# A constant group for eps in bn_aggr, and q's diagonal copies on GpSimd

## The chip, the cores and the metric

The kernel runs on one core of a Trainium2 chip. A core has five engines that run side by side, each with its own list of instructions taken strictly in order: TensorE (PE, matrix products; its weight loads appear as PEld), VectorE (DVE), ScalarE (ACT), GpSimd (POOL) and SyncE (SP), which here only starts transfers. Engines wait for each other on semaphores. The metric is the device time in microseconds (us) of one execution.

## The reference

The input x is 2048 tokens of 448 numbers in bf16. Six vectors of 448 (shift, scale and gate, twice) come from a small conditioning vector c. Then there are two residual blocks:

```python
mod = (_silu(c) @ w_mod).reshape(1, 6, 1, -1)      # sa, ca, ga, sb, cb, gb
h = _layernorm(x) * (1 + ca) + sa
x = x + ga * _A_ref(h, A_wqkv, A_wo)
h = _layernorm(x) * (1 + cb) + sb
x = x + gb * _B_ref(h, B_w_in, B_w_sp, B_b_sp, B_w_out)
```

Block A is attention with 16 heads of 28 numbers, in which a token sees itself and the 255 tokens before it. Block B multiplies by w_in (448 to 1792), applies gelu, splits into z1 and z2, normalizes z2 over its 896 numbers, mixes it over the tokens with a 2048x2048 matrix w_sp, adds b_sp, multiplies with z1 and multiplies by w_out (896 to 448). Each normalization is `(x - m) / jnp.sqrt(v + eps)` with eps = 1e-5, over 448 numbers in the two `h` and over 896 in z2, so each needs a mean and a variance for every token, 3 x 2048 in all.

## The kernel before

Tokens lie on the 128 partitions: 16 tiles of 128 tokens, in four blocks of four tiles (`tb`, 0 to 3). The work of each engine is written out as one list of small operations, `PLAN`. A word such as `d166` puts operation 166 on DVE; p is PE, a is ACT, d is DVE, t is POOL, s is SP. Each engine gets its operations in the order of the words. The class `Sched` turns what an operation depends on into semaphore waits, also on the engine's own earlier operations, PE's excepted. No planner runs when the program is built: the list alone sets the order.

**Statistics and normalization.** `stats` (L623) writes, for each tile, one `bn_stats` (L626; two for z2, by halves) and one `bn_aggr` (L629) on DVE, which gives mean and variance in `mv_all`. An addition of eps (L631) on DVE or POOL writes `ve_all`. POOL raises it to the power -0.5 (L633) into `rs_all`. `norm` (L636) applies both, on DVE in one operation (L644), or with a negated product of mean and `rs_all` first (L649, stored in `ve_all` too), and then an operation on POOL or DVE (L651). The three slots of `st_all`, `mv_all`, `rs_all` are those of the first norm, the second norm and z2. For z2 the operation that applies them is L1135.

**q, k, v.** The normalized rows `xn` of a block are transposed into `hT` by four transfers that SP starts (L467; for block 0 PE transposes), then scaled and shifted by DVE, POOL or ACT (L732 in blocks 1 to 3: four operations, each of which needs all four transfers). PE makes q (L763, block 0: L797), k (L821) and v (L841). ACT or DVE takes each out of PSUM (L772, L773, L802, L803 for q, L833 and L834 for k, L845 and L846 for v).

**q's diagonal blocks.** `QBD` is a second, block-diagonal layout of a part of q, with which PE scores a few keys of several heads in one matmul. For each block of tokens ACT fills it with zeros once per buffer (L521); there are two buffers, used by turns. Then four copies follow, one for each group of 32 partitions: 32 partitions x 256 elements in block 0 (L815 on ACT, L816 on DVE), 32 x 512 in the others (L790 on ACT, L791 on DVE). A copy needs all evictions of q of its block. Thirteen of the sixteen are on DVE, three on ACT. PE's L967, once per tile from tile 2 on, reads `QBD` and waits for all four copies of the tile's block: blocks 0, 1, 2 and 3 are first used at tiles 2, 4, 8 and 12.

**Attention and after.** For each tile PE makes scores (L956, L967; the first two tiles L926), ACT takes exponentials into `PW` (L912), DVE multiplies by a mask into `PT` (L975), PE multiplies with v (L1003), DVE divides (L1017, L1019), SP transposes `o_sb`, PE multiplies by wo (L1029), DVE adds to x (L1033). The second norm, its transposes (L467), the scaling L1054, the products L1123 (z2) and L1144 (z1) follow. When all of z2 is normalized, PE mixes over tokens (L1168) and multiplies by w_out (L1187); that is the last part, from 158 us on.

These lines hold the steps that the change touches: L623 to L657, L675 (`lock_q`), L782 to L791, L808 to L816, and `order` (L157).

Of the kernel before, what the change touches and what calls it, by code (L numbers as in the profile page):

```python
# [6 lines left out]
F32 = mybir.dt.float32  # L7
# [5 lines left out]
d24 d22 p47.1 p56.3 p48.2 p55.0 p57.1 p59.0 a0 a3 a5 a7 a9 d23 p37.1 p65.2 p71.3 p61.1 p49.0 p64.2 p50.3 p73.0  # L13
p46.3 p67.0 s1 s2 s4 d110 s6 s10 s8 a38 p42.0 p43 p44.1 p45 p70.2 p72.1 p60.2 t27 t28 t29 t32 t33 t30 d108
d111 t31 d109 t112 t113 t34 a100 t26 t102 t35 d115.3 d114.2 p124.7 d83 d82 p127.0 p75.0 a128 a129 d103 d125
d126 d118 d119 d116 d117 a104 p80.1 p77.0 p78.1 p76.2 p74.0 p52.3 p69.2 p68.0 s12 d182 d180 p62.1 t101 p51.0
p148.1 p81.2 p139.5 p140 p149 a150 p79.1 p54.2 a141 t106 t107 t105 p136.7 p137 a138 p63.2 t120 t121 d123.2
d122.0 p133.3 p130.6 p66.3 p53.0 p145.0 p146 p58.2 a131 d176 d183 d134 a135 s13 d243 d178 d177 d181 d179 t25
d184 t185 t191 t187 t189 d245 d41 d241 d186.3 s11 p142.7 p372.0 a132 p163.1 p170.6 p171 d244 p164 d165 a147
p151.0 p143 d144 d172 d247 p152 d153 a373.0 p378.0 p154.1 p155 d156 a39 a379.4 p397.0 a398.1 a399 a169 t36  # L20
d382 d374 d246 d166 d376 p157.7 p158 a159 s15 p90.1 p91 d92 d248 d84 d85 d242 d400 p93.0 p94 d95 d380 s193
t188.1 s194 t190.2 s195 t192.0 s196 d197 d200 p404.0 a405.5 p173.1 p174 a175 p160.7 p161 p375.0 p86.0 p87 d88
d198 d89 a406 a40 p425.0 a426.6.0 t249 t250 t254 d407 t252 t199 p377 p381 p383 d409 d384 d402 t253.2 d162
p217.0 p218 a219 a168 p210.1 p211 d212 p433.0 a434.0 p201.0 p202 a203 d167 p204.1 p205 a206 s14 d310 d385.2
p401.0 p403 p453.0 a454.2.1 s16 d430 s849 s259 t255.1 s260 d251.0 d256 d429 d436 d312 s386 s258 t257.3 s261
t97 t96 t262 t99 t263 t265 p226.0 p427.0 a428 p207.1 p227 p408 p208 d228 d306 p410 d411 d412.1 d307 s413 d98
d311 d435 a209 d215 d458 p461.0 p229.0 a462.1 d464 d214 d463 d457 p220.1 p221 p230 a231 p431.0 p432 s851
p481.0 p437 p438 d439 p223.0 p224 d225 d313 p455.0 a222 p232.1 d440.2 s441 d213 a482.3.2 d486 p489.0 d308 p233
d234 p235.0 p236 a456 a216 p483.0 p459.0 p460 a490.0 p508.0 d491 d492 d309 s21 s17 s852 p465 p466 d467 d485
d468.0 s469 a237 t264 p387.0 p388 d389 p414.1 p415 a484 p510.0 d416 t314 t315 a509.6.0 p536.0 a511 d390 d512  # L30
d391 p487.0 p488 p493 p494 p272.0 p538.0 d495 d496.1 a537.2.1 d541 d513 d540 p273 a274 p516.0 a517.5 p269.1
p275.0 p276 d277 p270 d271 p514.0 p515 a539 p564.0 a565.3.2 p282.0 p266.1 p267 a268 d519 p283 p566.0 a567 a284
d518 p520 t319 t320.1 s325 t321 t322.2 s326 d316.0 s323 t317 t318.3 s324 t330 d280 d417 d569 p544.0 a545.1
p442.1 p443 d444 d281 p521 d522 d523.0 p288.0 p289 a290 p291.1 p292 a293 p572.0 a573.5 p238.0 p239 d279 p294.1
p542.0 p295 p543 p592.0 a240 p470.0 p471 d445 d446 d546 d418 d419 d278 s20 s497 s848 s524 t392 t393 d547
d394.2 t395 s396 a296 a593.4.0 d568 p548 p549 p285.1 p594.0 p286 a287 p600.0 a601.2 d575 d472 p300.0 p301 a302
d550 d551.1 p570.0 p571 d596 d574 d473 p576 p577 p619.0 t420 t329 t327 d328 d597 p525.1 p337.0 p526 d578
d579.0 p598.0 a595 p599 p338 d603 d474 d527 a620.3.1 p627.0 d602 d528 d475 d421 d529 d530 t531 t447 t476
t422.0 t532 p340.1 p341 a339 s552 p553.0 p554 s18 p604 p605 a628.5 p647.0 a648.6.2 p621.0 a622 d342 p498.1
# [24 lines left out]
p1047.3 p1048 a1068 p1054.0 a1069 p1055.1 p1056 p1049 a1051 a1050 a1052 a1059 p1057 a1060 a1061 a1053 a1058
d1009 d992 d1002 d1008 d1001 d1010 d959 d1003 t1004 t1011 t1012 d880 d941 d952 d970 d977 d1013 d887 s846 s840
s845 s847 s838 s862 s839 s869 s863 s868 t1005 d1006 d988 t993 t994 d995 p1121.4 p1085.5 s837 p1070.1 d1071.1
d1122.0 t1072 p1082.2 p1124.4 t1123 p1076.7 d1077.0 t1078 d1083.0 t1084 p1115.3 d1116.0 t1117 s857 s854 s856
s867 s859 s861 s864 s855 s865 s860 s866 p1157.7 p1106.2 d1158.0 d1086.1 t1087 t820 t814 t1159 p1154.0 d1155.1
t1156 p1118.7 d1119.1 t1120 p1190.3 d1191.1 t1192 d1107.1 t1108 d1125.1 p1112.6 p1172.7 d1113.0 t1114 t1126
p1079.4 p1073.6 d1080.1 p1187.1 t816 t1081 d1074.0 t1075 d1173.0 p1109.6 p1148.2 p1088.4 p1175.0 p1184.7  # L70
d1089.1 t1090 d1110.1 p1094.4 p1181.6 t1111 p1130.5 t1174 d1188.0 p1178.1 d1095.3 d1149.1 p1127.2 d1131.0
t1189 d1179.0 p1136.3 p1097.1 p1091.4 t1180 d1176.0 s1132 d1137.0 t1150 p1139.5 s1096 d1185.1 d1128.3 t1186
d1092.2 s1093 d1182.1 t1183 d1140.1 t1141 p1103.4 d1104.1 s1105 d1098.1 s1129 s1099 p1142.7 p1151.5 p1145.0
d1143.1 t1144 d1146.1 t1177 p1201.2 p1100.1 t1147 p1197.4 d1152.0 t1153 s1138 d1101.0 s1102 p1202 d1203.0
s1204 p1205.0 p1206 d1207.2 s1208 p1160.3 p1163.6 d1164.0 d1161.1 s1162 s1165 p1193.5 p1194 p1198 d1195.3
s1196 p1133.2 d1199.0 d1134.2 s1135 s1200 p1166.5 d1167.3 s1168 p1169.3 d1170.1 s1171
"""


class Hold:  # L80


    def __init__(self, res):
# [1186 lines left out]
```

## Time and profile before

| what | value |
|---|---|
| device time, median of 3 runs | 282.59 us (282.34 to 283.21) |
| span of the profiled execution, first to last instruction | 279.0 us; no device time of that execution is given beside it |
| PE busy | 267.3 us (96%) |
| DVE busy | 164.5 us (59%) |
| POOL busy | 127.3 us (46%) |
| ACT busy | 121.4 us (44%) |
| copies into QBD on DVE | 13: 11 of 32x512, median 284 ns; 2 of 32x256, median 200 ns |
| additions of eps (L631) | 22 on POOL, median 232 ns; 15 on DVE, median 147 ns |

How to read the rows: L975 is line 975 of the kernel; `out<-in` names what an instruction writes and reads, x56 how many there are. A row of the timeline starts with its start and its length in us; several instructions of one kind that stand together are one row, and their lengths overlap a little, since an engine starts one before the one ahead has fully ended. `[1.02 <-DVE KT L834]` says that the engine was idle for 1.02 us before it and what ended the wait. SPq is SP's queue. A row of waits gives total us, times, longest. PE's busy time is modelled from its starts, so a busy PE is not PE at its peak.

### The profile page before, as it was taken

To read this page: it belongs to the slowest core of one execution; us is meant where nothing else is said; L and a number is where in the kernel's file an instruction comes from. 1 tells how busy PE (TensorE), PEld (TensorE's weight loads), DVE (VectorE), ACT (ScalarE), POOL (GpSimd) and SP (SyncE) were. 2 spreads that over 40 slices of the span, in tenths; PEclk is the share of its full clock that TensorE was granted. 3 is DMA by queue.
4 is the path that set the end of the run, shared out by engine and by line. 5 is a ranking of instruction groups with operands and counts; after the bars stand their busy time and mean duration, and the time that the engine had idled before them with its cause. 6 is when DMAs were issued, how large, how long until landed. Compare 5 with 4: busy or idle time off the path is not lost.

```text
span 279.0 us, 8426 instructions
## 1 busy us (share of the span) xinstructions
PE 267.3 (96%) x3741; PEld 155.6 (56%) x3751; DVE 164.5 (59%) x377; ACT 121.4 (44%) x142; POOL 127.3 (46%) x182
## 2 busy tenths in 40 slices
PE   7899998998999799999989899999999999999995
PEld 5786686677668676544545444444444444454552
DVE  3698999978999999938879501120212012153143
ACT  2399998899699789466755500000000000000000
POOL 7554567617364831596576503155363024062320
PEclk9999999999999999999999999999999999999999
DMA  7997953956632343659489996000000000102013
GB/s 203 294 238 136 147 100 97 121 93 97 126 62 50 98 80 61 179 89 150 99 153 192 212 182 130 0 0 0 2 1 0 0 2 0 33 16 62 0 39 115
DMA packets 67302, 25.55 MB, mean 92 GB/s; under 512 B 58497, under 2 KB 66178, under 8 KB 67266
## 3 DMA queue, kind: packets, MB, share of 16 engines
q1 hardware_dynamic: 66304, 24.21, 43.6%
q10 hardware_dynamic: 962, 0.80, 1.1%
q8 instruction: 29, 0.48, 0.7%
q14 instruction: 7, 0.06, 0.1%
HBM read 9.01 MB, written 1.84 MB: 39 GB/s over the span
## 4 chain that ended last, share of the span: by engine, by line
PE 53%; DVE 21%; POOL 12%; DMA 7%; ACT 3%; issue 2%; SPq 1%; POOLq 0%; DVEq 0%
PE ps L1168 34%; DVE PT L975 8%; PE ps L1187 8%; POOL rs_all L633 5%; DMA hT<-xn 5%; DVE st_all L626 3%; DMA wmodA<-in_w_mod_dram 2%; DVE o_sb L1019 2%; DVE x_sb L1033 2%; PE ps L763 2%; POOL hT L1054 2%; POOL ve_all L631 2%; PE ps L956 1%; PE ps L821 1%; PE ps L841 1%
## 5 line engine op out<-in xcount | busy, mean ns | idle before, releaser
L1175 POOL TENSOR_TENSOR z1T<-tmpg,z1T 128x512 bf16<-128x512 bf16 x28 | 32.0, 1152 | 74.5 <-DVE tmpg L1172 74.5
L1172 DVE TENSOR_TENSOR tmpg<-ps,bsp_bc 128x512 bf16<-128x512 f32 x28 | 19.0, 689 | 75.6 <-PE ps L1168 64.3
L912 ACT ACTIVATE PW<-ps 128x2048 bf16<-128x2048 f32 (+1 forms) x42 | 60.0, 1454 | 6.8 <-PE ps L956 5.2
L1168 PE MATMUL ps<-wspB,z 128*128 128x512 bf16 x219 | 49.7, 379 | 0.3
L1168 PE MATMUL ps<-wspA,z 128*128 128x512 bf16 x219 | 49.1, 379 | 0.9 <-DVE z L1135 0.7
L975 DVE TENSOR_TENSOR PT<-PW,mask 128x1024 bf16<-128x1024 bf16 x56 | 38.6, 714 | 0.1
L1168 PEld LDWEIGHTS ps<-wspA,z 128*128 128x128 bf16 x224 | 21.8, 98 | 27.2 <-DVE z L1135 1.0
L1168 PEld LDWEIGHTS ps<-wspB,z 128*128 128x128 bf16 x224 | 21.9, 98 | 26.2
L633 POOL TENSOR_TENSOR rs_all<-ve_all,neghalf 128x1 f32<-128x1 f32 (+2 forms) x37 | 24.5, 670 | 19.4 <-DVE ve_all L631 18.3
L1003 PE MATMUL ps<-Vaug,PT 128*128 128x32 bf16 x496 | 23.4, 177 | 1.3 <-DVE PT L975 0.7
L1003 PEld LDWEIGHTS ps<-Vaug,PT 128*128 128x128 bf16 x496 | 21.5, 96 | 3.9 <-DVE o_sb L1019 1.0
L1123 PE MATMUL ps<-w_in,hT 64*128 64x448 bf16 x224 | 22.0, 349 | 1.2 <-DVE st_all L626 1.2
L1144 PE MATMUL ps<-hT,w_in 64*128 64x512 bf16 x196 | 22.2, 376 | 0.0
L1187 PE MATMUL ps<-w_out_g,z1T 128*128 128x448 bf16 (+2 forms) x119 | 22.0, 342 | 0.0
L626 DVE BATCH_NORM_STATS2 st_all<-x_sb 128x6 f32<-128x448 bf16 x32 | 19.5, 617 | 3.0 <-DMA x_sb<-in_A_x_dram 2.8
L626 DVE BATCH_NORM_STATS2 st_all<-z 128x6 f32<-128x448 bf16 x32 | 18.5, 610 | 3.7 <-ACT z L1130 3.6
L1003 PE MATMUL ps<-Vaug,PW 128*128 128x32 bf16 x224 | 19.8, 176 | 0.0
L821 PE MATMUL ps<-hT,WQK 112*128 112x128 bf16 x256 | 17.4, 219 | 1.3 <-DVE KT L834 1.0
L1197 DVE TENSOR_TENSOR fin<-ps,x_sb 128x448 bf16<-128x448 f32 (+2 forms) x17 | 9.8, 595 | 14.7 <-PE ps L1187 9.9
L1003 PEld LDWEIGHTS ps<-Vaug,PW 128*128 128x128 bf16 x224 | 17.5, 96 | 1.1
L956 PE MATMUL ps<-qT,KT 32*128 32x128 bf16 (+5 forms) x1344 | 17.1, 197 | 1.0 <-DVE KT L834 0.9
L1130 ACT ACTIVATE z<-ps 128x896 bf16<-128x896 f32 x16 | 13.9, 914 | 9.3 <-PE ps L1123 6.8
(104 smaller groups left out, 361.8 us busy)
## 6 DMA issues: line engine op xcount, KB each, us to landing
out_dram<-fin SPq DMA_DIRECT2D x15, 112.0 KB, 1.7
wmodB<-in_w_mod_dram SPq DMA_DIRECT2D x1, 1568.0 KB, 14.9
x_sb<-in_A_x_dram SPq DMA_DIRECT2D x3, 448.0 KB, 9.0
w_in<-in_B_w_in_dram SPq DMA_DIRECT2D x3, 448.0 KB, 4.5
w_out_g<-in_B_w_out_dram SPq DMA_DIRECT2D x1, 784.0 KB, 5.0
bsp_bc<-in_B_b_sp_dram SPq DMA_DIRECT2D x1, 512.0 KB, 5.2
x_sb<-in_A_x_dram SPq DMA_DIRECT2D x2, 224.0 KB, 5.1
hT<-xn SPq DMA_TRANSPOSE x28, 3.2
```

The costliest lines, as they stand in the source:

```text
L626: st = [dve(0.62 if True else 0, lambda e, t=t, ci=ci, s=s: e.bn_stats(st_all[:, slot, t, ci, :], s()), deps(t), prio) for ci, s in enumer ...
L633: return pool(0.4 + 0.15 * len(tiles), lambda e: e.tensor_tensor(rs_all[:, slot, a:b], ve_all[:, slot, a:b], neghalf[:, 0:b - a], ALU.pow) ...
L821: km = lambda g, kc, start, stop, h=h, t=t: lambda e: e.matmul(ps[:, h.slot[0], g * 128:(g + 1) * 128], lhsT=WQK[0:CP, kc, 16 + 4 * g:20 + ...
L912: ex = act(xdur, lambda e, out_ap=out_ap, in_ap=in_ap: e.activation(out_ap(), in_ap(), ACT.Exp, scale=SCALE), [s] + list(after), v - 8.0 + ...
L956: fm.append(lambda e, hm=hm, qi=qi, key=key, kn=kn, lo=lo, hi=hi, col=col, p0=p0, t=t, j=j: e.matmul(ps[p0:p0 + kn, hm.slot[t], col:col + ...
L975: return lock_d(0.68, lambda e: e.tensor_tensor(cols(hp.slot[0] * 2048 + 1024 * k, [[256, 4], [128, 2], [1, 128]]), cols(at_w() + pad + at ...
L1003: fns.append(lambda e, hp=hp, hO=hO, hi=hi, bi=bi, kb=kb, hd=hd, nb=nb, a=at[hi][bi], p_of=p_of: e.matmul(ps[:, hO.slot[0], 32 * hd:32 * h ...
L1123: return lambda e, kc, p0, start, stop: e.matmul(ps[:, hs[t % 2].slot[hf], 0:D], lhsT=hT[p0:p0 + 64, kc, t * 128:(t + 1) * 128], rhs=w_in[ ...
L1144: return lambda e, kc, p0, start, stop: e.matmul(ps[:, hs[b // 2].slot[b % 2], :], lhsT=w_in[p0:p0 + 64, kc, ft * 128:(ft + 1) * 128], rhs ...
L1168: m = pe(16 * MMS, [lambda e, h=h, si=si, ft=ft, tb=tb: e.matmul(ps[:, h.slot[0], :], lhsT=z2[:, si, ft * 128:(ft + 1) * 128], rhs=(wspA i ...
L1175: u = pool(1.16, lambda e, ht=ht, ft=ft, tb=tb: e.tensor_tensor(z1T[tb][:, ft, :], tmpg[:, ht.slot[0], :], z1T[tb][:, ft, :], ALU.mult), [ ...
L1187: return [lambda e, ft=ft: e.matmul(ps[:, h.slot[0], 0:hi - lo], lhsT=z1T[t // 4][:, ft, (t % 4) * 128:(t % 4 + 1) * 128], rhs=w_out_g[:, ...
```

## The change

Two edits. First, eps no longer has an operation of its own. `bn_stats` leaves groups of three numbers (count, mean, sum of squares about the mean), and `bn_aggr` joins groups. The statistics of a tile now lie in 15 numbers; the last three are a constant group with count 0, mean 0 and a sum of squares of n times eps (n is 448 or 896), set once at the start by three memsets on DVE. `bn_aggr` reads 9 numbers (15 for z2) and its variance already holds eps. All 37 additions go, and POOL's L633 waits for `bn_aggr` itself. The negated products get a tile of their own, `nm_all`.

Second, the thirteen copies into `QBD` that were on DVE are on POOL. They use 32 of the 128 partitions; an operation so marked (`part`) waits for the operation ahead of it in POOL's list, and the one behind waits for it. The three copies on ACT stay.

`PLAN` keeps the order of its words apart from the operations that are gone or new; `d` became `t` for the thirteen copies, and all numbers are counted anew. So PE's, ACT's and SP's lists are what they were. DVE's list loses the thirteen copies and 15 additions and gains three memsets. POOL's loses 22 additions and gains the copies at these places: one ahead of the first block's three `xn` operations (L651, tiles 5 to 7); one between the `xn` operations of the next block; three ahead of the last scaling L732 of block 2; four behind the scaling L732 of block 3 and ahead of the first `rs_all` of the second norm; of the last four one ahead of an `xn` operation of the second norm (L651), two behind it, and one behind a copy L657, ahead of an `rs_all`.

```diff
+        self.part = False
...
-            self.prog[op.eng].append(op)
+            prog = self.prog[op.eng]
+            if op.eng == "pool" and prog and (op.part or prog[-1].part):
+                op.deps.add(prog[-1])
+            prog.append(op)
...
-    st_all, _, _ = alloc("st_all", [128, 3, NT, 2, 6], F32)
+    st_all, _, _ = alloc("st_all", [128, 3, NT, 15], F32)
-    ve_all, _, _ = alloc("ve_all", [128, 3, NT], F32)
+    nm_all, _, _ = alloc("nm_all", [128, 3, NT], F32)
...
+    t_eps = [dve(0.1, lambda e: e.memset(st_all[:, :, :, 12:14], 0.0), prio=-98.0),
+             dve(0.1, lambda e: e.memset(st_all[:, 0:2, :, 14:15], D * EPS), prio=-98.0),
+             dve(0.1, lambda e: e.memset(st_all[:, 2:3, :, 14:15], FH * EPS), prio=-98.0)]
...
-            st = [dve(0.62 if True else 0, lambda e, t=t, ci=ci, s=s: e.bn_stats(st_all[:, slot, t, ci, :], s()), deps(t), prio)
+            n = len(srcs(t))
+            st = [dve(0.62, lambda e, t=t, o=12 - 6 * (n - ci), s=s: e.bn_stats(st_all[:, slot, t, o:o + 6], s()), deps(t), prio)
                   for ci, s in enumerate(srcs(t))]
-            n = len(st)
-            aggr.append(dve(0.2, lambda e, t=t, n=n: e.bn_aggr(mv_all[:, slot, t, :], st_all[:, slot, t, 0:n, :]), st, prio - 0.01))
+            aggr.append(dve(0.2, lambda e, t=t, n=n: e.bn_aggr(mv_all[:, slot, t, :], st_all[:, slot, t, 12 - 6 * n:15]), [st, t_eps], prio - 0.01))
-        fe = lambda e: e.tensor_scalar(ve_all[:, slot, a:b], mv_all[:, slot, a:b, 1], EPS, None, ALU.add)
-        ve = add({"dve": (0.16, fe), "pool": (0.23, fe)}, aggr, prio)
-        return pool(0.4 + 0.15 * len(tiles), lambda e: e.tensor_tensor(rs_all[:, slot, a:b], ve_all[:, slot, a:b], neghalf[:, 0:b - a], ALU.pow),
-                    [ve, t_nh], prio - 0.01)
+        return pool(0.4 + 0.15 * len(tiles), lambda e: e.tensor_tensor(rs_all[:, slot, a:b], mv_all[:, slot, a:b, 1], neghalf[:, 0:b - a], ALU.pow),
+                    [aggr, t_nh], prio - 0.01)
...
     def lock_q(*a):
-        return locks(either(*a))
+        op = locks(free(*a))
+        op.part = True
+        return op
```

More of the change, by code (lines that the diff above doesn't have):

```diff
@@ L18 @@
[L18 to L27, printed above, removed]
@@ L73 @@
[L73 to L76, printed above, removed]
+d24 d22 p50.1 p59.3 p51.2 p58.0 p60.1 p62.0 a0 a3 a5 a7 a9 d23 d25 d26 d27 p40.1 p68.2 p74.3 p64.1 p52.0 p67.2
@@ new lines @@
+p53.3 p76.0 p49.3 p70.0 s1 s2 s4 d113 s6 s10 s8 a41 p45.0 p46 p47.1 p48 p73.2 p75.1 p63.2 t30 t31 t32 t35 t36
+t33 d111 d114 t34 d112 t115 t37 a103 t29 t105 t38 d117.3 d116.2 p125.7 d86 d85 p128.0 p78.0 a129 a130 d106
+d126 d127 d120 d121 d118 d119 a107 p83.1 p80.0 p81.1 p79.2 p77.0 p55.3 p72.2 p71.0 s12 d183 d181 p65.1 t104
+p54.0 p149.1 p84.2 p140.5 p141 p150 a151 p82.1 p57.2 a142 t109 t110 t108 p137.7 p138 a139 p66.2 t122 d124.2
+d123.0 p134.3 p131.6 p69.3 p56.0 p146.0 p147 p61.2 a132 d177 d184 d135 a136 s13 d243 d179 d178 d182 d180 t28
@@ new lines @@
+a451 a216 p477.0 p454.0 p455 a484.0 p501.0 d485 d486 d308 s21 s17 s834 p460 p461 d462 d479 d463.0 s464 a237
+t263 p385.0 p386 d387 p411.1 p412 a478 p503.0 d413 t313 a502.6.0 p528.0 a504 d388 d505 d389 p481.0 p482 p487
+p488 p271.0 p530.0 d489 d490.1 a529.2.1 d533 d506 d532 p272 a273 p509.0 a510.5 p268.1 p274.0 p275 d276 p269
+d270 p507.0 p508 a531 p555.0 a556.3.2 p281.0 p265.1 p266 a267 d512 p282 p557.0 a558 a283 d511 p513 t317 t318.1
+s323 t319 t320.2 s324 d314.0 s321 t315 t316.3 s322 t328 t279 d414 d560 p536.0 a537.1 p438.1 p439 d440 t280
@@ new lines @@
+p595 a617.5 p635.0 a636.6.2 p610.0 a611 d340 p492.1 p493 d547 p296.0 p297 a298 t471 d596 d597.2 d612 p614.0
+d613 s835 s571 s598 d494 t419 s420 d640 d548 d619 d549 d618 d495 t443 t444 t445.1 t446 s447 p662.0 a663.0.0
+d667 p615 p332.0 p333 a334 p329.1 p330 a331 d639 t343 t472.2 d473 s474 p643.0 a644.1 p599.0 p600 p637.0 a638
+p345.1 p346 p620 a347 d601 d602 t344 d645 d666 t342 p670.0 a671.2 p621 p664.0 d622 d496 p348.0 p349 a350
+p357.1 p358 t550 t551 t552.0 t804 d623.2 s624 p689.0 d646 d673 d525.2 p302.0 p303 d304 d672 s19 p641.0 p642
@@ new lines @@
+p1004.0 p1005.1 p1006 p1007 a1011 a1009 a1010 a1008 t860 t794 s795 t818 d817 t816 d891 d815 d881 d939 d927
+d899 d928 d945 t914 t876 d877 d921 t908 d909 t882 d923 p948.2 p949.3 p950 p951 p964.1 p965.0 p966 a952 d929
+d953 d954 a958 d959 d955 d883 d960 t892 t956 d893 t940 p967 a968 a974 p1028.3 p1029.1 p1030 p1031 t866 t930
+t946 t924 t800 a1032 a1033 p1012.2 p1013.3 p1014 a1034 p1020.0 a1035 p1021.1 p1022 p1015 a1017 a1016 a1018
+a1025 p1023 a1026 a1027 a1019 a1024 d976 d961 d970 d975 d969 d977 d931 d971 t978 d861 d915 d925 d941 d947 d979
@@ new lines @@
+d867 s828 s822 s827 s829 s820 s844 s821 s851 s845 s850 t972 d973 d957 t962 d963 p1087.4 p1051.5 s819 p1036.1
+d1037.1 d1088.0 t1038 p1048.2 p1090.4 t1089 p1042.7 d1043.0 t1044 d1049.0 t1050 p1081.3 d1082.0 t1083 s839
+s836 s838 s849 s841 s843 s846 s837 s847 s842 s848 p1123.7 p1072.2 d1124.0 d1052.1 t1053 t802 t796 t1125
+p1120.0 d1121.1 t1122 p1084.7 d1085.1 t1086 p1156.3 d1157.1 t1158 d1073.1 t1074 d1091.1 p1078.6 p1138.7
+d1079.0 t1080 t1092 p1045.4 p1039.6 d1046.1 p1153.1 t798 t1047 d1040.0 t1041 d1139.0 p1075.6 p1114.2 p1054.4
@@ new lines @@
+p1141.0 p1150.7 d1055.1 t1056 d1076.1 p1060.4 p1147.6 t1077 p1096.5 t1140 d1154.0 p1144.1 d1061.3 d1115.1
+p1093.2 d1097.0 t1155 d1145.0 p1102.3 p1063.1 p1057.4 t1146 d1142.0 s1098 d1103.0 t1116 p1105.5 s1062 d1151.1
+d1094.3 t1152 d1058.2 s1059 d1148.1 t1149 d1106.1 t1107 p1069.4 d1070.1 s1071 d1064.1 s1095 s1065 p1108.7
+p1117.5 p1111.0 d1109.1 t1110 d1112.1 t1143 p1167.2 p1066.1 t1113 p1163.4 d1118.0 t1119 s1104 d1067.0 s1068
+p1168 d1169.0 s1170 p1171.0 p1172 d1173.2 s1174 p1126.3 p1129.6 d1130.0 d1127.1 s1128 s1131 p1159.5 p1160
@@ L77 @@
+p1164 d1161.3 s1162 p1099.2 d1165.0 d1100.2 s1101 s1166 p1132.5 d1133.3 s1134 p1135.3 d1136.1 s1137
 """
@@ L647, in norm @@
         else:
-            nm = ve_all[:, slot, t:t + 1]
+            nm = nm_all[:, slot, t:t + 1]
             fm = lambda e: e.tensor_scalar(nm, m, z, -1.0, ALU.mult, ALU.mult)
```

84 lines of the change are left out of this document (32 added, 52 removed).

## The prediction

> **What bounds the kernel now.** I read the page first (busy shares), then the chain that ended last in order of time, busy time by stage, PE's waits, and the timeline of each engine around the instructions that move.
>
> ```profile
> span 279.0 us, 8426 instructions
> PE 267.3 (96%) x3741; PEld 155.6 (56%) x3751; DVE 164.5 (59%) x377; ACT 121.4 (44%) x142; POOL 127.3 (46%) x182
> 44.00:64.00 20.00, 20.00 (x608) 15.03 (x606) 18.33 (x41) 17.61 (x19) 9.85 (x13) 1.00 0.70 117
> 64.00:111.00 47.00, 44.73 (x1340) 32.75 (x1342) 44.76 (x95) 40.37 (x39) 23.05 (x33) 1.00 0.44 81
> 158.10 10.74 PE ps L1168 x49
> ```
>
> From 158.10 us on, TensorE (PE) works through a fixed list to the end, so the result is decided by how late it reaches that row. Before it, attention (about 28 to 111 us) has PE, VectorE (DVE) and ScalarE all nearly full. In 44 to 64 PE is busy 20.00 of 20.00 us (in the two rows by stage: length, then PE, PEld, DVE, ACT and POOL busy), in 64 to 111 DVE 44.76 of 47.00. So work taken off DVE can help only after 64, and any pause of PE in 44 to 64 is lost. These are PE's own waits, nearly all that a gain could come from after 28 us (in us: total, times, longest):
>
> ```profile
> PE ps L1123 <- DVE st_all L626: 1.2, 1, 1.2
> PE ps L821 <- DVE KT L834: 1.0, 1, 1.0
> PE ps L956 <- DVE KT L834: 0.9, 1, 0.9
> PE ps L1168 <- DVE z L1135: 0.7, 1, 0.7
> PE ps L1003 <- DVE PT L975: 0.7, 1, 0.7
> PE ps L1003 <- DVE o_sb L1019: 0.6, 1, 0.6
> ```
>
> **The change, part by part.** I keep one running number: how late PE is against the trace above. The prices first.
>
> ```profile
> L791 DVE COPY QBD<-qT x11: 269/284/753, 38.3 to 93.0; 32x512 bf16<-32x512 bf16 x11
> L615 POOL COPY WQK<-wq_st x5: 556/560/561, 8.3 to 11.3; 112x448 bf16<-112x448 bf16 x5
> L657 POOL COPY xn<-xn x13: 231/238/2659, 65.1 to 136.5; 128x64 bf16<-128x64 bf16 x13
> L975 DVE TENSOR_TENSOR PT<-PW,mask x56: 615/681/1411, 32.1 to 112.7; 128x1024 bf16<-128x1024 bf16 x56
> L631 POOL TENSOR_SCALAR ve_all<-mv_all x22: 208/232/921, 5.1 to 155.5; 128x1 f32<-128x1 f32 x18, 128x2 f32<-128x2 f32 x2, 128x4 f32<-128x4 f32 x2
> L629 DVE BATCH_NORM_AGGREGATE mv_all<-st_all 128x2 f32<-128x6 f32 x32 | 5.2, 170 | 0.3
> L629 DVE BATCH_NORM_AGGREGATE mv_all<-st_all 128x2 f32<-128x12 f32 x16 | 2.7, 186 | 0.0
> 63.15 0.75 POOL L631 TENSOR_SCALAR ve_all<-mv_all 128x1 f32<-128x1 f32 x1
> 63.99 0.57 POOL L633 TENSOR_TENSOR rs_all<-ve_all,neghalf 128x1 f32<-128x1 f32 x1
> ```
>
> Rows by source line give min/median/max in ns. GpSimd (POOL) copies 448 elements a partition in 0.56 us and 64 in 0.23, that is 0.85 ns an element, so the copy of 512 costs 0.61 us and that of 256 0.39 us. The lower bound is DVE's own 0.28, the upper one what a stretched copy shows (2.66). I take 0.61, nearest the 448-element row. POOL waiting for itself costs 0.1 us: L631 ends at 63.90, L633, which reads it, starts at 63.99 (start and length lead the timeline's rows).
>
> *Eps by a constant group.* 37 additions go, 22 on POOL and 15 on DVE. bn_aggr reads 9 or 15 numbers in place of 6 or 12; six more cost 16 ns, so three cost 8, and 48 times 8 ns is 0.4 us, taken as nothing apart from DVE's savings. Three memsets stand in DVE's list before the first statistics, while DVE waits for x: nothing; without that cover, 0.3 us. Below nothing they can't go. What the missing additions are worth is in step 5.
>
> *The copies.* Thirteen leave DVE and stand in POOL's list. PE, ACT and SP keep their lists, so it matters what POOL's in-order list then holds up.
>
> *Step 1, first block (two copies of 256).* The first copy now stands ahead of POOL's xn x3 and needs all four evictions of q.
>
> ```profile
> 19.04 2.10 POOL L651 TENSOR_SCALAR xn<-x_sb,rs_all,ve_all 128x448 bf16<-128x448 bf16 x3
> 21.75 0.68 DVE L803 CAST qT<-ps 128x512 bf16<-128x512 f32 x1
> 18.46 6.18 SPq L467 DMA_TRANSPOSE hT<-xn  x4
> DMA to landing us min/median/max: 2.5/3.3/4.0
> 25.89 0.74 DVE L732 TENSOR_SCALAR hT<-hT,modT 112x512 bf16<-112x512 bf16 x2
> 28.14 1.05 PE L821 MATMUL ps<-hT,WQK 112*128 112x128 bf16 x16
> ```
>
> The copy starts after 21.75+0.68=22.43, and xn at about 23.0 in place of 19.04. Three xn at 0.70 follow; SP issues a transpose per 1.3 us, so three more start at 23.8, 25.1, 26.4. The last of before ran to 18.46+6.18=24.64 and landed about 25.9, just when DVE's L732 began: no slack. (The landing row is of the last two.) Now it lands at 26.4+2.5=28.9. Behind SP's three queue a load of x, wo_g and a transpose of wspA, which have slack. DVE stands still at L732, its three scalings (two in the 0.74 of that row, a third after a short copy) take an estimated 1.3 us, and PE's L821 starts at 30.3, not 28.14: **2.2 late**. Bounds: 2.0 (a copy as short as DVE's) to 4.6 (4.0 to land, xn stretched).
>
> *Step 2, second block (three copies of 512).*
>
> ```profile
> 43.51 1.07 PE L821 MATMUL ps<-hT,WQK 112*128 112x128 bf16 x16 [1.02 <-DVE KT L834]
> 43.97 0.27 DVE L791 COPY QBD<-qT 32x512 bf16<-32x512 bf16 x1
> 44.41 0.38 PE L967 MATMUL ps<-QBD,KT 128*128 128x256 bf16 x2
> 44.03 1.45 POOL L732 TENSOR_SCALAR hT<-hT,modT 112x512 bf16<-112x512 bf16 x1
> ```
>
> PE's wait of 1.02 absorbs some, since DVE has shed copies: 1.2 late at 43.51. But L967 needs every copy of its block; DVE finished at 44.24, PE used it at 44.41. On POOL the three stand where the last L732 began, 44.03, and POOL's stage is some 1.9 late from step 1 (its last xn waits for DVE, late by 2.2 less one copy): 44.03+1.9+3x0.61+0.3=48.1. PE's L967 starts at 48.2: **3.8 late**, and PE is full until 64. Bounds: 2.2 (POOL's scalings unstretched) to 6.
>
> *Step 3, third block (four copies).*
>
> ```profile
> 57.40 0.28 DVE L791 COPY QBD<-qT 32x512 bf16<-32x512 bf16 x1 [1.19 <-ACT qT L772]
> 52.03 2.37 ACT L912 ACTIVATE PW<-ps 128x2048 bf16<-128x2048 f32 x2
> 54.62 1.28 DVE L975 TENSOR_TENSOR PT<-PW,mask 128x1024 bf16<-128x1024 bf16 x2
> 61.80 1.27 POOL L732 TENSOR_SCALAR hT<-hT,modT 112x512 bf16<-112x512 bf16 x1 [7.70 <-DMA hT<-xn]
> 64.59 0.40 DVE L644 TENSOR_SCALAR xn<-x_sb,mv_all,rs_all 128x448 bf16<-128x448 bf16 x1 [0.79 <-POOL rs_all L633]
> ```
>
> DVE loses four copies and the 1.19 wait, 1.19+4x0.28=2.3 us, and then stands at L644, which waits for POOL's rs. All four copies lie between L732 and that rs: 4x0.71=2.8 more, the addition L631 (63.15 to 63.99, 0.84 with its gap) less: **2.0**. DVE comes to this place about 3.1 late, not 3.8, as its masks at 54.62 follow ACT's exponential of 52.03 (about 1.9 of the 2.37, the rest a small one) with 0.7 us of slack; so 5.1, and PE's next L1003 waits for DVE. Bounds of the step: 0.7 to 3.
>
> *Step 4, fourth block (four copies), 66 to 111.*
>
> ```profile
> 81.02 1.08 ACT L772 ACTIVATE qT<-ps 128x512 bf16<-128x512 f32 x2
> 93.78 2.66 POOL L657 COPY xn<-xn 128x64 bf16<-128x64 bf16 x1
> 95.48 0.38 PE L967 MATMUL ps<-QBD,KT 128*128 128x256 bf16 x2
> ```
>
> Here DVE is the bound and saves 1.1 us: four copies of 0.28, an estimated 0.4 of waits for additions, less 0.4 for an xn on POOL held behind the copy that needs q (ready at 82.10). But the last copy stands behind L657, which ran to 96.44, and L967 wants it at 95.48. At worst it ends 97.2, 1.9 late against a PE that is then 0.7 earlier; at best nothing. I take 1.0. Sum 5.1-1.1+1.0=5.0.
>
> *Step 5, 111 to 158.*
>
> ```profile
> 153.17 0.77 POOL L631 TENSOR_SCALAR ve_all<-mv_all 128x1 f32<-128x1 f32 x2
> 155.53 0.92 POOL L631 TENSOR_SCALAR ve_all<-mv_all 128x1 f32<-128x1 f32 x1
> ```
>
> The additions on POOL are on the way here: 1.7 us before the last rs, so PE's wait of 0.7 at L1168 goes; PE's own L1144 is then what is late. Some 1.0 more goes ahead of the last transpose, out of PE's 1.2 at L1123. **Gain 1.7**, bounds 0 to 1.9.
>
> **Sum:** 2.2, less 1.0 absorbed, plus 2.6 (to 3.8), plus 1.3 net to 5.1, minus 1.1, plus 1.0, minus 1.7: 3.3 late. Against the profiled span that is 282.3. The page has no device time of its own; the median of the runs shown, 282.59, stands 3.6 above the span, so 282.6+3.3=**285.9 us**.
>
> [...]
>
> **Rivals.** *Faster:* POOL's copies are hidden and DVE's 3.7 us (thirteen at 0.28) count. For it speaks POOL's 46%; against it, the zero slack at 25.89 and 44.41. It decides whether xn stays before about 20 us. PE's waits on DVE of 0.9, 0.7, 0.6 and 0.7 would go: 279.7. Chance 0.10.
>
> *Blocking:* each POOL copy also stops DVE for its whole length. For it speak L791 at 753 against 269, L975 at 1411 against 615 beside POOL work; against it, most L975 at 681. If the three and four copies of steps 2 and 4 stop DVE, 7x0.61 less their 7x0.28 is 2.3 more: 288.2. Chance 0.15. [...]
>
> *Nothing moves:* the waits are absorbed and only step 5 offsets them, within 0.3%: 0.05. That the additions would not go is excluded by the new program's lists.
>
> **How the numbers follow.** My forecast has 0.70. All lower bounds at once (1.0, 2.2, then 1.5+0.7, -1.1, -1.9) would be 281.8, all upper ones (3.6, 6, then 5.3+3, -1.1+1.9, 0) 291.7; its own range is half of the way to either, 283.8 to 288.8. The whole range goes further, to 289.5 for the blocking case (288.2) with a longer step 1, and to 283.0; left out are the faster case, nothing-moves and a little above. Less than 0.3% (0.85 us) can't be told from no change. Slower 0.85, same 0.05, faster 0.10.
>
> **What would show it.** Step 1: xn on POOL starting near 23, L732 on DVE with a DMA wait of 2 to 3 us, L821 near 30. Step 2: L967 with a wait on POOL's QBD near 48. Step 3: DVE's L644 with a wait on rs of several us. Step 5: no wait at L1168 above 0.3 us. If xn runs before 20 us, or PE shows no wait for POOL at QBD, I am wrong; if the late PE is caught up before 111, there is slack that I don't see.

## The result and the profile after

The changed kernel takes 291.4 us (median; 290.78 to 293.29), the kernel before 282.46 (281.82 to 283.21) beside it: ratio 1.036, 95% interval 1.030 to 1.043. That is 8.9 us slower by the medians. I had predicted 285.9 us and 283.0 to 289.5: the direction was right, and the time lies above the range.

First the page after: its span, busy times, and the row of the granted clock, which had a 9 in every slice before.

```profile
span 289.7 us, 8407 instructions
PE 272.5 (94%) x3751; PEld 157.0 (54%) x3751; DVE 160.9 (56%) x352; ACT 121.9 (42%) x142; POOL 123.0 (42%) x173
PEclk9999699799979999999999999999999999999999
```

DVE and POOL both have less work than before (164.5 and 127.3): DVE lost copies and additions, and the additions that POOL lost took more than the copies that it got. The kernel is slower all the same. PE's busy time has grown from 267.3 to 272.5 us with the same list of products (ten more of them were recorded in this trace). The clock row says why: in three places the granted clock is below full. I hadn't looked for that at all.

PE's waits after, as far as they are new, and two of DVE's (us: total, times, longest; line numbers have moved by some 5: L826 was L821, L972 was L967, L1173 was L1168, L737 was L732, L796 was L791, L647 was L644, L558 was L553):

```profile
PE ps L826 <- DVE modT L558: 4.4, 1, 4.4
PE ps L972 <- POOL QBD L796: 4.0, 1, 4.0
PE ps L826 <- DVE x_sb L1038: 1.3, 1, 1.3
DVE hT L737 <- DMA hT<-xn: 4.3, 1, 4.3
DVE xn L647 <- POOL rs_all L636: 4.8, 2, 4.0
```

The waits for the last additions, 1.2 us at the z2 product and 0.7 at the mixing, are gone, and PE has two pauses of 4 us instead. The first is step 1 of the prediction. Timelines of all engines after, around it:

```profile
21.97 0.68 DVE L808 CAST qT<-ps 128x512 bf16<-128x512 f32 x1
22.81 0.42 POOL L821 COPY QBD<-qT 32x256 bf16<-32x256 bf16 x1 [3.88 <-DVE qT L808]
23.34 2.86 POOL L654 TENSOR_SCALAR xn<-x_sb,rs_all,nm_all 128x448 bf16<-128x448 bf16 x3
18.36 9.82 SPq L469 DMA_TRANSPOSE hT<-xn  x4
30.81 1.12 DVE L737 TENSOR_SCALAR hT<-hT,modT 112x512 bf16<-112x512 bf16 x2 [4.25 <-DMA hT<-xn]
32.58 0.14 DVE L558 TENSOR_SCALAR modT<-ps 128x4 f32<-128x4 f32 x1
32.87 1.86 PE L826 MATMUL ps<-hT,WQK 112*128 112x128 bf16 x16 [4.41 <-DVE modT L558]
```

The copy stands and waits 3.88 us for q; behind it `xn`, the transposes, DVE's scalings and PE's L826 all follow. L826 ran 1.05 us for its 16 products before and 1.86 now. The second pause is step 2:

```profile
48.92 1.96 POOL L737 TENSOR_SCALAR hT<-hT,modT 112x512 bf16<-112x512 bf16 x2
51.01 2.81 POOL L796 COPY QBD<-qT 32x512 bf16<-32x512 bf16 x3
53.97 0.38 PE L972 MATMUL ps<-QBD,KT 128*128 128x256 bf16 x2 [3.99 <-POOL QBD L796]
```

What the pauses do to PE afterwards stands in the windows of the changed kernel (length, then busy us of PE, PEld, DVE, ACT and POOL, granted clock, DMA share, GB/s):

```profile
32.00:37.00 5.00, 4.13 (x68) 2.73 (x68) 2.98 (x8) 1.01 (x2) 2.34 (x3) 0.50 0.84 169
50.00:54.00 4.00, 0.03 (x1) 0.06 (x2) 2.35 (x5) 1.44 (x2) 3.64 (x6) 1.00 0.77 214
54.00:58.00 4.00, 4.00 (x103) 2.85 (x104) 1.33 (x3) 2.47 (x2) 3.70 (x6) 0.57 0.40 61
77.00:81.00 4.00, 2.23 (x89) 2.00 (x88) 3.97 (x8) 3.41 (x4) 3.61 (x4) 1.00 0.19 42
81.00:86.00 5.00, 4.66 (x104) 2.94 (x104) 3.87 (x10) 1.97 (x2) 0.00 (x0) 0.66 0.76 173
```

Behind each pause PE has work and runs it at a lower clock. The 0.57 and 0.66 are means over a window: in the trace's record the granted clock is 0.50 from 30.50 to 37.32 us, from 54.39 to 57.80 and from 81.70 to 85.11, and 1.00 in between. The first of these begins while PE still waits. The third time there was no pause of 4 us ahead, only a stretch with PE busy 2.23 of 4.00 us.

### The profile page after: what moved, and what is told of

Read it like the earlier page. It is cut to its first block, busy times and chain, and to the rows that moved or that the text cites. A ratio compares the mean times of both kernels' runs of the same rounds, so it can differ in the third digit from the quotient of the medians.

```text
span 289.7 us, 8407 instructions
## 1 busy us (share of the span) xinstructions
PE 272.5 (94%) x3751; PEld 157.0 (54%) x3751; DVE 160.9 (56%) x352; ACT 121.9 (42%) x142; POOL 123.0 (42%) x173
## 4 chain that ended last, share of the span: by engine, by line
PE 72%; POOL 8%; DVE 7%; issue 7%; DMA 3%; ACT 2%; SPq 0%; POOLq 0%; DVEq 0%
PE ps L1173 33%; PE ps L1128 7%; PE ps L1149 7%; PE ps L1192 7%; PE ps L1008 3%; PE ps L1034 3%; POOL xn L654 3%; PE ps L961 2%; DVE PT L980 2%; PE ps L826 2%; DMA wmodA<-in_w_mod_dram 2%; POOL QBD L796 2%; PE ps L768 2%; PE ps L846 2%; ACT PW L917 1%
## 5 line engine op out<-in xcount | busy, mean ns | idle before, releaser
L1173 PE MATMUL ps<-wspB,z 128*128 128x512 bf16 x224 | 50.1, 379 | 0.0
L1173 PE MATMUL ps<-wspA,z 128*128 128x512 bf16 x224 | 49.5, 379 | 0.0
L1173 PEld LDWEIGHTS ps<-wspA,z 128*128 128x128 bf16 x224 | 21.8, 98 | 26.6 <-issue 0.4
L1173 PEld LDWEIGHTS ps<-wspB,z 128*128 128x128 bf16 x224 | 21.9, 98 | 26.2
L636 POOL TENSOR_TENSOR rs_all<-mv_all,neghalf 128x1 f32<-128x1 f32 (+2 forms) x37 | 23.9, 665 | 28.7 <-DVE mv_all L634 28.5
L826 PE MATMUL ps<-hT,WQK 112*128 112x128 bf16 x256 | 18.2, 225 | 6.1 <-DVE modT L558 4.4
L826 PEld LDWEIGHTS ps<-hT,WQK 112*128 112x128 bf16 x256 | 15.7, 100 | 7.7 <-POOL xn L654 4.5
L1157 ACT ACTIVATE z1T<-ps 128x512 bf16<-128x512 f32 x28 | 14.6, 603 | 9.1 <-PE ps L1149 9.1
L961 PE MATMUL ps<-qT,KT 32*128 32x128 bf16 (+5 forms) x1344 | 18.1, 202 | 0.1
```

The lines of the kernel that those rows point to most:

```text
L636: return pool(0.4 + 0.15 * len(tiles), lambda e: e.tensor_tensor(rs_all[:, slot, a:b], mv_all[:, slot, a:b, 1], neghalf[:, 0:b - a], ALU.pow),
L826: km = lambda g, kc, start, stop, h=h, t=t: lambda e: e.matmul(ps[:, h.slot[0], g * 128:(g + 1) * 128], lhsT=WQK[0:CP, kc, 16 + 4 * g:20 + ...
L961: fm.append(lambda e, hm=hm, qi=qi, key=key, kn=kn, lo=lo, hi=hi, col=col, p0=p0, t=t, j=j: e.matmul(ps[p0:p0 + kn, hm.slot[t], col:col + ...
L1173: m = pe(16 * MMS, [lambda e, h=h, si=si, ft=ft, tb=tb: e.matmul(ps[:, h.slot[0], :], lhsT=z2[:, si, ft * 128:(ft + 1) * 128], rhs=(wspA i ...
```

## How lateness is counted below

PE's list is the same in all kernels here (the dummy products of three of them left out), so the same instruction can be compared from trace to trace. PE's entry into attention scatters: its first scores of tile 2 (L956 before, at 27.23 us) come between 1.1 us earlier and 3.2 later from kernel to kernel, in no order of the edits. The first loads of weights, which land sooner or later, have a part in it (the last row is of the kernel with block 3's copies on POOL: PE waits 2.1 us, and with block 2's not at all); whether they explain all of it wasn't followed. The other two rows are the kernel before and the changed kernel:

```profile
27.23 0.61 PE L956 MATMUL ps<-qT,KT 32*128 32x128 bf16 x48
27.45 0.61 PE L961 MATMUL ps<-qT,KT 32*128 32x128 bf16 x48
PE ps L549 <- DMA wmodA<-in_w_mod_dram: 2.1, 1, 2.1
```

So I count how late PE is against the kernel before, less that first difference. The table has this lateness in us: at the L826 of step 1, at the first `QBD` product of tiles 2, 4, 5, 9 and 14, and at the first product of the mixing (L1168 before, at 158.10 us; L1173 in the changed kernel, at 168.56). The last column is the measured ratio to the kernel before with its interval.

| kernel | L826 | tile 2 | 4 | 5 | 9 | 14 | mixing | ratio |
|---|---|---|---|---|---|---|---|---|
| changed kernel | 4.5 | 6.4 | 9.3 | 10.4 | 13.2 | 12.6 | 10.2 | 1.036 (1.030 to 1.043) |
| eps group only | -0.1 | 0.0 | 0.0 | 0.0 | -0.4 | -0.5 | -2.6 | 0.988 (0.983 to 0.994) |
| copies only | 4.7 | 7.0 | 8.7 | 10.1 | 12.6 | 12.3 | 12.6 | 1.044 (1.038 to 1.050) |
| + first copy | 4.8 | 6.3 | 6.3 | 6.3 | 5.5 | 5.4 | 3.3 | 1.007 (1.002 to 1.011) |
| + block 1's three | 0.4 | 0.3 | 3.2 | 4.0 | 3.1 | 3.1 | 0.9 | 1.000 (0.996 to 1.003) |
| + block 2's four | -0.1 | 0.0 | 0.0 | 0.0 | 2.7 | 2.6 | 0.5 | 0.995 (0.991 to 0.999) |
| + block 3's four | -0.1 | 0.0 | 0.1 | 0.0 | -0.2 | -1.3 | -3.4 | 0.985 (0.980 to 0.990) |
| one word moved | -0.1 | 0.0 | 1.7 | 2.7 | 5.4 | 4.6 | 2.5 | 1.015 (1.007 to 1.022) |
| all placed anew | -0.1 | 0.0 | -0.7 | -0.7 | -1.5 | -1.9 | -4.1 | 0.984 (0.978 to 0.989) |
| first fill | 12.7 | 12.6 | 15.6 | 15.6 | 16.2 | 15.6 | 14.4 | 1.047 (1.040 to 1.053) |
| second fill | 4.5 | 4.4 | 7.4 | 7.4 | 8.4 | 7.4 | 6.0 | 1.024 (1.015 to 1.033) |
| first copy, filled | 4.6 | 4.5 | 4.5 | 4.5 | 4.7 | 4.5 | 3.1 | 1.013 (1.007 to 1.020) |

The rows with a plus have the eps group and only the named copies on POOL. The lateness at the mixing is that of one profiled execution, the ratio that of all runs: for the changed kernel they agree (0.036 of 282.46 is 10.2 us), for the others they differ by up to 2 us, where the half widths of the intervals are 0.9 to 2.5 us.

## The experiments

My theory after reading the trace: the copies' places make PE pause, the pauses make its clock fall, and both cost. The rivals: the eps group is what hurts; a copy costs by itself, wherever it stands; the waits alone count and the low clock is hidden.

**The two parts.** One kernel has the changed list with the thirteen words given back to DVE:

```diff
-d246 t167 d374 ...
+d246 d167 d374 ...
```

> The changed kernel with its thirteen copies given back to DVE at the places they had before: the constant group for eps alone. If the copies on POOL carry the whole loss and the missing additions are worth what PE waits for them (1.2 us at L1123 and 0.7 us at L1168 in the kernel before), it takes 280.6 to 282.0 us, below the 282.5 of before. If the constant group costs something that I took as nothing (bn_aggr over 9 and 15 numbers, three memsets, POOL started later by DVE), it is slower than before: above 283.3.

Measured: 278.8 us, ratio 0.988. The eps group alone is a gain, 2.6 us of PE's lateness, 2.1 of it behind tile 14. No cost of the longer `bn_aggr` shows. The time came out below the range of the expectation: I had expected a gain of up to 1.9 us, and the ratio's interval says 1.8 to 4.9.

The other kernel is the one before with the thirteen words on POOL and the waits around them; eps is added as before.

> The kernel before with the thirteen copies alone on POOL; all 37 additions of eps stay. If the two parts add up, it takes the 291.4 us of the changed kernel and the 1 to 2 us that the additions cost on top: 291.5 to 293.5. If the constant group were what hurts, it would stay near 283.

Measured: 294.2 us, ratio 1.044; that is 0.7 above my range. The copies cost 12.6 us at the mixing, the eps group gives 2.6: the sum is 10.0, the changed kernel has 10.2. So the two edits add up, and the first rival falls.

**The copies one block at a time.** Each kernel is the eps group with one group of words on POOL, for instance:

```diff
 # block 1 only
-d215 d453 p456.0 ... d459 d214 ... s437 d213
+t215 d453 p456.0 ... d459 t214 ... s437 t213
```

> The constant group, and of the copies only the first (the one ahead of POOL's xn x3 in block 0) on POOL; the other twelve on DVE. Against 278.8 us with all copies on DVE. If this one copy makes PE pause over 4 us at L826 and PE's clock is then granted at half for some 5 us, most of the changed kernel's loss is here: 284 to 288 us, with a granted clock near 0.5 behind the pause. If the place is worth only the 2.2 us that I had predicted, with PE at full clock behind it and part of it absorbed by PE's later waits, it takes 280 to 281.5.

Measured: 284.6 us. One copy of 0.42 us makes PE pause 4.7 us and then run at half clock (`PEclk9999599999999999...`), 6.3 us late at tile 2, as the first theory had it. From tile 9 on a part is absorbed, and at the mixing 5.9 us is left against the eps group alone: the time is at the lower edge of the first theory's range and far above the other's.

> The constant group, and only block 1's three copies (32x512, ahead of the last scaling of block 2) on POOL; the first block's are back on DVE, so POOL isn't late when it comes to them. By my step 2 without the 1.9 us that step 1 handed on, L972 of tile 4 starts some 1.9 us late: 280 to 281.5 us, a pause below 4 us and the clock near 1.00. If the three copies are stretched to some 1 us each beside VectorE, as in the changed kernel, the pause is 3 us or more and the time 282 to 284.

Measured: 281.7 us, with a pause of 4.0 us. Against the eps group alone PE gets 3.2 us late at tile 4 and 4.0 at tile 5. Rows of this kernel, the price of the copies (min/median/max in ns) and PE's wait:

```profile
L796 POOL COPY QBD<-qT x3: 603/953/1100, 43.6 to 45.8; 32x512 bf16<-32x512 bf16 x3
46.57 0.59 PE L972 MATMUL ps<-QBD,KT 128*128 128x256 bf16 x2 [3.99 <-POOL QBD L796]
```

The three are stretched, 2.7 us in place of 1.8, although step 1 hands nothing on here. So the pause is that of the second guess, over 3 us, and the clock falls behind it (0.50 from 46.18 to 49.59 us); the time lies between the two guesses.

> The constant group, and only block 2's four copies (ahead of the first rs_all of the second norm) on POOL. By my step 3 PE gets 2.0 us later (0.7 to 3): 279.5 to 281.8 us. If the late rs_all is absorbed, since DVE has time to spare by then, it stays at 278.8, within 0.9. If POOL is the bound from there on, over 282.

Measured: 280.7 us; 3.1 us late at tile 9 against the eps group alone, a little above my 0.7 to 3. PE waits 1.3 and 0.8 us there, and in the profiled run the clock falls behind these short waits too (0.50 from 70.47 to 73.89 us). The four copies have the price that I had given them, 0.61 us:

```profile
L796 POOL COPY QBD<-qT x4: 604/604/612, 62.4 to 64.4; 32x512 bf16<-32x512 bf16 x4
```

> The constant group, and only block 3's four copies on POOL, around an xn of the second norm. By my step 4 (net nothing: DVE gains 1.1 us, the place loses 1.0) it stays at 278.8 us, within 0.9. If the copy that waits for q at the head of the second norm's xn holds up the last tiles, 279.7 to 281.

Measured: 277.6 us, a little below the band of the first guess. These four gain 0.8 us at tile 14 and at the mixing against the eps group alone. The four parts give 5.9+3.5+3.1-0.8=11.7 us on top of the eps group; all thirteen copies together give 12.8. The four parts hold twelve copies: the second one of block 0 was in none of them.

**The places.** The changed kernel with one word moved, the first copy behind the `xn` operations rather than ahead:

```diff
-d246 t167 d374 ... t188.1 s194 t190.2 s195 t192.0 s196
+d246 d374 ... t188.1 s194 t190.2 s195 t192.0 t167 s196
```

> The changed kernel with one word of its list moved: the first copy of block 0 stands behind POOL's xn x3, not ahead of them. The single-part runs add up: with the first copy alone on POOL PE ends 6.0 us later than with all on DVE. If the parts add up, this one word takes 6 us away: 285.4 us, with one pause of about 4 us left, at L972 of tile 4. If the later pauses only absorb what the first one leaves (PE waits there for something that isn't late itself), less than 3 us goes: over 288.5.

Measured: 284.9 us, beside 280.1 for the kernel before in that series; ratio 1.015 against 1.036, 2.1% or 6.0 us. By the trace it is 7.7 us at the mixing. One word carries most of the loss. PE's remaining pause at L972 is 2.4 us, not 4. The difference wasn't handed on by the first pause: with block 1's copies alone there is no first pause either, and PE waits 3.99 us. In that kernel POOL waits for the block's transposes until 39.62 us before it can begin the scalings ahead of the copies, and with the one word moved only until 36.41 (the starts differ by 0.1). What brings the transposes forward wasn't followed.

Then all thirteen copies on POOL, at places chosen so that the work behind them isn't needed soon: block 0's two behind the `xn` of tiles 5 to 7, block 1's behind a `wo_g` product and ahead of the next block's scalings, block 2's behind an `xn` operation, block 3's behind an `xn` of the second norm.

> The changed kernel with the thirteen copies still on POOL, at other places of its list: in block 0 both behind the xn x3 of the second block, in block 1 behind a late copy of wo_g and ahead of nothing but the scaling of the next block, in block 2 behind an xn, in block 3 behind an xn of the second norm. If the places are what costs (a copy that waits for all of q holds up xn, the scalings and rs_all behind it), most of the loss goes: 279 to 284 us, and L826 and L972 show no wait above 1.5 us. If a copy on POOL costs by itself (0.61 us and two waits for itself, or DVE slowed beside it), it stays above 287.

Measured: 276.5 us, ratio 0.984: 5.7 us less than the 282.2 of the kernel before beside it, so it is below both the kernel before and the changed kernel, and below my range too. Its profile has the waits and the chain that I would have wished for the change (PE's waits; then the shares of the chain that ended last):

```profile
PE ps L568 <- DVE one L489: 1.1, 1, 1.1
PE ps L549 <- DMA wmodA<-in_w_mod_dram: 0.7, 2, 0.4
PE ps L1008 <- issue: 0.6, 1, 0.6
PE ps L826 <- DVE st_all L632: 0.5, 1, 0.5
PE 88%; DVE 4%; ACT 3%; DMA 3%; issue 1%; SPq 1%
L796 POOL COPY QBD<-qT x11: 602/612/1110, 36.3 to 82.9; 32x512 bf16<-32x512 bf16 x11
```

The copies cost here what they cost in the changed kernel, each with its waits, and PE gets 4.1 us earlier. So here the price of a copy on POOL doesn't matter; its place does, and the second rival falls.

**The clock.** To tell the pauses from the clock behind them, PE gets dummy products in the pauses. The waits for data stay.

```diff
+    bK = View(banks, [(5,)])
+    for _ in range(76):
+        hW = Hold(bK)
+        op = pe(0.12, [lambda e, hW=hW: e.matmul(ps[:, hW.slot[0], 0:256]..., lhsT=fill[:], rhs=fill[:]...)], [t_fill], 2000.0, [hW])
+        hW.until.append(op)
```

> The changed kernel with dummy work on PE: 40 products of 128x256 into an unused bank of PSUM ahead of the L826 that waits 4.4 us for the scaled hT, and 36 ahead of the L972 of tile 4 that waits 4.0 us for QBD (about 4 us of work each at full clock; nothing reads what they write). The waits for data are as they were; PE only isn't idle in them. If a pause of some 4 us makes the granted clock fall to 0.5 for the next 4 to 6 us, and that costs time, the clock stays at 1.00 from 32 to 38 and 54 to 58 us and the time falls by 2.5 to 4 us, to 287.4 to 288.9. If the waits alone carry the loss and the lower clock is hidden behind the other engines, it stays at 291.4, within 0.9, or rises by what the dummy work is longer than the waits.

Measured: 294.7 us, slower, and no verdict: my first 40 products were put on a bank of PSUM whose last reader is a DVE eviction, and that stands behind the scalings which DVE was waiting to do. PE waited for it and ran the dummies only then:

```profile
PE ps L1220 <- DVE Vaug L857: 6.5, 1, 6.5
35.85 6.26 PE L1220 MATMUL ps<-fill 128*128 128x256 bf16 x40 [6.47 <-DVE Vaug L857]
```

L826 got 12.7 us late in place of 4.5, through the experiment's own fault. Again with a bank that ACT empties early:

```diff
-    bK = View(banks, [(5,)])
+    bK = View(banks, [(5,), (7,)])
```

> The changed kernel with the same dummy products as in the run with the fill before, but the 40 ahead of L826 now write a bank of PSUM that ACT has emptied by 26 us, so that they can start where PE's pause starts, at 28.5 us, and lie in it (40 of about 0.11 us, 4.3 us, against a pause of 4.4). If the fall of the granted clock to 0.5 behind a pause costs time, the clock stays at 1.00 from 32 to 58 us, L972 of tile 4 comes 2 us earlier against the changed kernel and the end 2 to 4 us: 287.4 to 289.4 us. If the low clock is hidden behind the waits for the other engines, it stays within 0.9 of 291.4.

Measured: 286.7 us beside 280.1 for the kernel before; ratio 1.024. The clock row has a 9 in every slice. The stretches that match those above (windows of this kernel):

```profile
31.00:35.00 4.00, 4.00 (x47) 3.62 (x48) 1.28 (x4) 2.14 (x2) 1.21 (x2) 1.00 0.69 171
35.00:39.00 4.00, 3.98 (x80) 2.54 (x78) 3.64 (x10) 1.53 (x3) 2.26 (x3) 1.00 0.94 204
55.00:59.00 4.00, 4.00 (x122) 2.94 (x123) 1.82 (x4) 2.49 (x3) 3.70 (x6) 1.00 0.71 76
77.00:81.00 4.00, 2.37 (x97) 2.13 (x89) 3.97 (x8) 3.39 (x4) 3.19 (x4) 1.00 0.29 66
81.00:86.00 5.00, 5.00 (x156) 3.25 (x153) 4.58 (x13) 3.33 (x3) 0.34 (x1) 1.00 1.02 141
```

L826 comes as late as in the changed kernel (4.5), since the wait for data is the same; but at tile 2 PE is 4.4 late in place of 6.4, at tile 5 7.4 in place of 10.4, at the mixing 6.0 in place of 10.2. With 8.6 us of useless work (4.53 and 4.10) the kernel is faster: 1.2% by the ratios, whose intervals overlap a little, and 4.2 us by the trace. It isn't one lucky execution: the mean granted clock is 0.971 to 0.976 in all four runs of the changed kernel and 0.999 to 1.00 in all four of this one. That is what the low clock cost, and for the changed kernel the third rival falls. At the third place (77 to 86 us) no dummy products stand; the clock stayed full there too (1.00 in both rows), and the last section has its busy times.

> The constant group and only the first copy on POOL (one pause of 4.7 us, 6.3 us late at tile 2, of which 4.7 is the pause by my count and some 1.6 the clock), with the 40 dummy products in the pause. If the clock costs 1.6 us, tile 2 is 4.7 us late in place of 6.3 and the time 1.6 us shorter than without them; if not, it is as late as without them.

Measured: 284.2 us. At tile 2 it is 4.5 late in place of 6.3, as expected, but at the mixing 3.1 in place of 3.3, and the time is no shorter. Where there is only one pause, PE's later waits take up what the clock cost, as the third rival had it. In the changed kernel the next pause comes before the last loss is made good: its lateness stays at 10.4 us from tile 5 to tile 8 and goes up again at tile 9.

## Why the prediction was wrong

The direction and the mechanism were right: the first copy holds up `xn` (forecast at 23.0, came at 23.34), L972 waits for POOL's `QBD`, L647 waits for rs, and there is no wait at the mixing. The size was not. My running number beside the two runs that split it:

| after step | predicted | clock kept full | changed kernel |
|---|---|---|---|
| 1 (tile 2) | 2.2 | 4.4 | 6.4 |
| 2 (tile 5) | 3.8 | 7.4 | 10.4 |
| 3 (tile 9) | 5.1 | 8.4 | 13.2 |
| 4 (tile 14) | 5.0 | 7.4 | 12.6 |
| 5 (mixing) | 3.3 | 6.0 | 10.2 |

Of the 6.9 us between 3.3 and 10.2, 4.2 are the clock and 2.7 are sizes: 2.2 too little in step 1 and 1.4 in step 2, then 0.3 and 0.9 too much in steps 3 and 4, and 0.3 too large a gain in step 5.

**The clock was no term of the sum.** Every step took PE's work behind a pause at the durations of before. The rows of before couldn't show otherwise: PE's longest wait there is 1.2 us. In the changed kernel full clock returned at 37.32, 57.80 and 85.11 us, each time behind 3.41 us in which PE was busy throughout (from 33.91, 54.39 and 81.70). Ahead of the first fall PE was still busy 1.38 of 3.41 us and ahead of the second 0.42, and the third had no long pause at all (2.02; last section). I had priced a first pause of 2.2 us and didn't ask what the clock does behind it; with one word moved, a pause of 2.36 us had half clock behind it, from 45.33 to 48.74 us.

**Step 1, 2.2 forecast, 4.4 measured, is the term that was mis-sized.** From the rows above: `xn` began 0.3 later than I said (0.2 of that is the start) and took 2.86, not 2.10; from its end at 26.20 to the landing, where DVE's L737 begins, 4.6 us passed, where I had 3.8 (25.1 to 28.9); and from there to L826 2.06, where I had 1.4, since the three scalings, with a short copy between them, took until 32.66, 1.85 us and not my estimated 1.3 (L558, on which the wait is put, ends 0.06 later). That is 0.3, 0.8, 0.8 and 0.7, all on the same side. My bounds had named two of the four, the landing and a stretched `xn`; all four together come to about the upper bound of 4.6. What stretched `xn` and the landing wasn't tried; the second fill, which has the same order, has `xn` at 2.86 again.

**Step 2, 1.6 on top forecast, 3.0 measured.** The three copies with their waits took 2.81 us where I had 2.13 (2.63 with the clock kept full), and POOL's list came to them later. DVE had two mask products at that moment. The first took 0.69 us, about the median of before, 0.68, the second 1.10:

```profile
50.98 1.71 DVE L980 TENSOR_TENSOR PT<-PW,mask 128x1024 bf16<-128x1024 bf16 x2 [0.44 <-ACT PW L917]
```

In block 2 DVE stood still during the copies, and my price of 0.61 held (604 to 612 ns). In the changed kernel's block 1 the two copies that started while a mask product ran took 1.13 and 0.96 us, the third, without one, 0.60. Not every meeting stretches the copy: the last copy of the changed kernel, at 105.83 us, started 0.16 ahead of a mask product and took 0.60, and the mask product took 0.99.

**Steps 3 to 5 came within 0.9 us** with the clock out of the way: +1.0 for +1.3, -1.0 for -0.1, -1.4 for -1.7. The eps group alone gave 2.6, more than the 1.7 of step 5.

**The rivals.** The blocking case, 288.2 us, was nearer to the time but isn't what happened: with the copies on POOL the mean of DVE's 56 mask products is 718 ns, and it was 714 before. Where they met in step 2, copies took up to 1.13 us and mask products up to 1.10, but they met in few places, and there DVE isn't what PE waits for. The faster case gave 279.7 if copies were hidden; the newly placed kernel shows that case and goes below it, at 276.5. Its condition, `xn` before 20 us, is just what the one moved word restores.

**The range.** I had all upper bounds at 291.7 and cut the range half way, as if the steps' errors would partly cancel. The two large ones, of steps 1 and 2, lay on the same side, and the clock stood in no bound at all. That 291.4 lies just below 291.7 is luck.

The chain that ended last after has this row at the place where 158.10 stood before:

```profile
168.63 76.08 PE ps L1173 x352
```

## What to carry to other kernels

Moving a short operation to an engine with an in-order list cost here what stood behind it, not what it takes (one copy of 0.42 us, 5.9 us at the mixing): ask for each moved word what its operand waits for, and put it behind the work that others need. Where a change makes a full PE pause, price the pause and then the clock behind it (here 4.2 of the 10.2 us at the mixing), and let the upper bounds of steps whose lateness adds up add up too. Before an edit is given up, try its list with the moved words somewhere else: here, beside the eps group alone, the same thirteen copies cost 13 us at one set of places and gained 1.5 at another (by the traces; the gain is within the intervals of the ratios).

## What the runs showed of the hardware

- **The clock fell behind short waits too.** With only block 2's copies on POOL there is no pause over 1.3 us, and yet the clock falls in the profiled run. Two of the three stretches of half clock in the changed kernel last 3.41 us (54.39 to 57.80 and 81.70 to 85.11), so PE's busy time is read here in stretches of that length. Two of the block 2 kernel, then two of the second fill:

```profile
67.06:70.47 3.41, 1.74 (x43) 1.64 (x44) 3.38 (x7) 2.78 (x3) 2.74 (x3) 1.00 0.38 79
70.47:73.89 3.42, 3.42 (x77) 2.05 (x78) 2.82 (x7) 1.72 (x1) 0.00 (x0) 0.50 0.56 148
76.05:79.46 3.41, 2.56 (x79) 1.94 (x78) 3.32 (x7) 2.84 (x4) 2.91 (x5) 1.00 0.20 43
79.46:82.87 3.41, 2.62 (x99) 2.01 (x96) 3.38 (x7) 1.67 (x4) 0.73 (x1) 1.00 0.54 134
```

  In the block 2 kernel the waits of 1.25 and 0.78 us both end in one such stretch, PE is busy 0.51 of it, and the next has half clock. In the second fill the waits, 0.85 and 0.79 us, fall in two stretches, 0.75 and 0.77 busy, and the clock stays at 1.00 (82.87 to 86.29 too). In the changed kernel PE was busy 0.40, 0.12 and 0.59 of the 3.41 us ahead of its three falls. How little work it takes for a fall wasn't tried. The same waits don't cost a fall in every run: of the eight runs of the block 2 kernel four have a mean clock of 0.999 to 1.00, the other four 0.993 to 0.994.
- **GpSimd copies on 32 partitions.** 512 elements took 604 to 612 ns while DVE stood still (block 2's copies alone on POOL), and 1.13 us beside one of DVE's mask products (51.01 us in the changed kernel), 1.20 with the one word moved; DVE's own copy is 284, the median before. The wait for itself between two of them added about 0.06 us (four of 0.604 in 2.61).
